# Expert slots: one PSUM bank after the other, and a new order of relu, split and load

## The chip, the cores and the metric

The program runs on one core of one Trainium2 chip, as one launch. A core has five engines with a queue each, worked through strictly in order: TensorE (PE; its weight loads are listed apart as PEld), VectorE (DVE), ScalarE (ACT), GpSimd (POOL) and SyncE (SP), which here issues most of the transfers. They wait for each other through semaphores. The metric is the device time of one execution in microseconds; lower is better.

## The reference, cut to what matters

Three layers follow each other: a chunked attention, a mixture of eight experts in which each token goes to one expert, and a dense layer with a rational activation. The change lies in the second:

```
logits = x @ w_gate + modality_bias[modality_id]      # 3072 tokens, 512 wide
e_idx = argmax(logits)
for e in range(8):                                    # only experts that have tokens
    mask = e_idx == e
    h = maximum(x[mask] @ w1[e], 0)                   # 512 -> 1024
    out[mask] = gate_w[mask, None] * (h @ w2[e])      # 1024 -> 512
...
h = x @ w_in; h2 = h * h; h3 = h2 * h                 # third layer, 512 -> 2048
P = a0 + a1 h + a2 h2 + a3 h3;  Q = 1 + |b0||h| + |b1| h2
return (P / (Q + 1e-6)) @ w_out                       # 2048 -> 512
```

## The kernel before, in words

**Slots.** The router sorts the tokens by expert and packs them into slots of 128; a slot belongs to one expert. Slots 0 and 1 are worked off in `second`, and the first product of slot 2 too; from then on the loop in `moe` runs passes i = 3 to 26. Pass i makes the first products of slot i (`mm1`), the hidden rows of slot i-1 (`prep_h`), and the second products and the output of slot i-1 (`mm2`, `out`). Slots 0 to 25 hold tokens.

**One pass on TensorE.** `mm1` multiplies 128 tokens (in two parts, `h` and `l`, high and low, so that the product keeps float32 precision) with `w1`, also in two parts, `w1h` and `w1l`: 24 matmuls of 128x512 into the two banks of the PSUM tile `pb`, both banks alternating. Between them stand the 8 transposes of `prep_h(i-1)`, which turn the relu'd rows `hs` for the second product. Then 4 transposes of `prep_x(i+1)`, the next slot's tokens, and 24 matmuls of `mm2(i-1)` into a bank of `pa`.

**The other engines in one pass.** ScalarE copies `prep_h`'s results to `hh`, makes the relu (`hs`, two halves, one a bank; every transpose of `prep_h` needs both), copies the next tokens (`xs`), and rounds new weights to their high part (`split_hi`, four pieces of 128x1024). VectorE makes the low parts (`hl`, `xs` low, `split_lo`). `out` scales the result on ScalarE.

**New weights.** When a slot's expert differs from that of the slot before it, `load_w` (SP, under an If on a flag) fetches four pieces of 512 KB into `w1r` or `w2r`, and `split_w` (ACT and DVE, under the same flag) makes the parts. `w1` of slot i+2 is asked for in pass i and split in pass i+1; `w2` of slot i is asked for in pass i and split in pass i+1. The next load into the same tile waits until the split has read it. In this data the expert changes at slots 12, 13 and 17; slot 12 is an expert with one slot.

**Filler.** The weights of the third layer are converted in 33 steps, hung into the passes: one step after `mm2` in each pass, a second one before `load_w(i, w2r)` while i < 12, the rest in pass 25. Step n splits piece n-1 (`pair`: a CAST on ACT to `wih` or `wo`, and a subtraction on DVE), asks on SP for piece n+1 into the half of `wr` that `pair` has just read, and works on piece n (`bits`: an ACTIVATE on ACT that waits for piece n to land, four instructions on DVE). The second kind of piece leaves through POOL to the tensor `wod`.

**The order** of every queue is that of the source (`manual_schedule`); the framework puts in the semaphores. In the last pass the first 512 result rows are prepared for the third layer (`Rows.prep`): two tiles of them through `pb`.

Of the kernel before, what the change touches and what calls it, by code (L numbers as in the profile page):

```python
# [12 lines left out]
F32 = mybir.dt.float32  # L13
# [33 lines left out]
def attention(nc, tc, ex, ident, q, k, v, wg_d, mod, mbias, pos_u, out_u, constants):  # L47
# [8 lines left out]
    with ExitStack() as ctx:  # L56
# [56 lines left out]

        def scores(t):
            qt, kt = qs[t % NB_IN], kz[t % NB_IN]
            sc = ex.pa[:, t % 2]
            for hp in range(HP):
                for c in range(TC):
                    x = c // 2 * KP + c % 2 * CH
                    nc.tensor.matmul(  # L120
                        sc[CH * c:CH * c + CH, hp * P:hp * P + P], lhsT=qt[:, hp, CH * c:CH * c + CH], rhs=kt[:, :, hp, x:x + 64],
                        start=True, stop=True,
                    )
            sc_t[t] = sc.rearrange("p (h k) -> p h k", k=64)
# [36 lines left out]
        def pv(t):  # L161
            s = pT_t.pop(t)
            w = vz[t % NB_IN]
            ps = ex.pb
            n = 2 * (D + 1)
            for hp in range(HP):
                for c in range(TC):
                    nc.tensor.matmul(
                        ps[CH * c:CH * c + CH, hp // 2, hp % 2 * n:hp % 2 * n + n], lhsT=s[:, hp, CH * c:CH * c + CH], rhs=w[:, :, hp, c, :],
                        start=True, stop=True,  # L170
                    )
            o = ps[:, :, 0:2 * n].rearrange("p g (h d) -> p g h d", d=D + 1)
            rs = wk.tile([P, 2, HP], F32, tag="rs", name="rs")
            V.tensor_scalar_add(rs, o[:, :, :, D], 1e-9)
            chore()
            V.reciprocal(rs, rs)
            chore()
            x = xp.tile([P, H, D], F32, tag="x", name="x")
            V.tensor_tensor(
                out=x.rearrange("p (g h) d -> p g h d", g=2), in0=o[:, :, :, 0:D],  # L180
                in1=rs[:, :, :, None].to_broadcast([P, 2, HP, D]), op=ALU.mult,
            )
            (nc.gpsimd if t < NT - 3 else nc.sync).dma_start(out=xd[row(t):row(t) + P, :], in_=x.rearrange("p h d -> p (h d)"))
            chore()
            x_t[t] = x
# [106 lines left out]
class Router:  # L292
# [226 lines left out]
    def second(self):  # L519
# [7 lines left out]
        ex.mm1_0(0, 3)  # L527
        ps = self.rank(n, NT)
        ex.prep_x0(1)
        ex.relu(0)  # L530
        ex.mm1_0(1, 0, 1, 2, 3)
        rest = self.first_rest()
        for f in rest[:2]:
# [47 lines left out]
        some = self.wk.tile([P, 32], F16, tag="rs", name="some")  # L581
        V.tensor_scalar(out=some, in0=tb, scalar1=0.0, scalar2=None, op0=ALU.not_equal)
        V.tensor_scalar(out=f[:, 1], in0=tb, scalar1=0.0, scalar2=-1.0, op0=ALU.is_gt, op1=ALU.mult)
        ex.relu(1)
        cnt = self.tp.tile([P, 32], F32, tag="t", name="cnt")
        ex.mm2_0(0, 0)
        nc.tensor.matmul(cnt, lhsT=self.ones, rhs=some, start=True, stop=True)
# [6 lines left out]
        ex.load_w(EARLY, ex.w1r, ex.w1v)  # L594
        ex.split_w(EARLY, ex.w1r, ex.w1h, ex.w1l)
        ex.load_w(EARLY + 1, ex.w1r, ex.w1v)
        for part in range(3):
            ex.mm1(EARLY, part)
            if part < 2:
                ex.prep_h0(1, part)  # L600
        for step in (*rest[2:], *self.terms(n, NT), *self.gates(n, NT), *self.gate_parts()):
            step()
        bg = self.wk.tile([P, NT, 3, 32], F16, name="bg", bufs=1)
# [1 line left out]
        V.tensor_tensor(  # L605
            out=bg, in0=be.rearrange("p s t -> p t s")[:, :, None, :].to_broadcast(SG), in1=self.g16[:, :, :, None].to_broadcast(SG), op=ALU.mult,
        )
        ex.relu(EARLY)
        low = ex.prep_x(EARLY + 1)
        ex.mm2_0(1, 0)  # L610
        low()
# [44 lines left out]
class Experts:  # L656


    def __init__(self, nc, tc, ident, xd, yd, w1, w2, src_u, pos_u, out_u, gate_s, flags):
        self.nc, self.tc, self.ident = nc, tc, ident  # L660
        self.xd, self.yd, self.src_u, self.pos_u, self.out_u, self.gate_s, self.flags = xd, yd, src_u, pos_u, out_u, gate_s, flags
        self.w1v = w1.rearrange("e (p k) f -> (e p) (k f)", k=4)
        self.w2v = w2.rearrange("e (p j) d -> (e p) (j d)", j=8)
        self.hps, self.yps, self.hT = {}, {}, {}
        self.ctx = ExitStack()
        self.sp = self.ctx.enter_context(tc.tile_pool(name="shared", side="right", bufs=1))
        self.ps = self.ctx.enter_context(tc.tile_pool(name="shared_ps", side="right", bufs=4, space=PSUM))
        self.pa = self.ps.tile([P, 2, 512], F32, name="pa", bufs=1)
        self.pb = self.ps.tile([P, 2, 512], F32, name="pb", bufs=1)
        self.hs = self.sp.tile([P, 8, P], F32, name="hs")  # L670
        self.xs = [self.sp.tile([P, 2, 4, P], F32R, name=f"xs{i}") for i in range(2)]
        self.xg = [self.sp.tile([P, D_M], F32, name=f"xg{i}") for i in range(3)]
        self.ys = self.sp.tile([P, D_M + 1], F32, name="ys")
        self.e0 = self.sp.tile([1, 1], I32, name="e0")
        self.w1r = self.sp.tile([P, 4, 1024], F32, name="w1r")
        self.w1h = self.sp.tile([P, 4, 1024], F32R, name="w1h")
        self.w1l = self.sp.tile([P, 4, 1024], F32R, name="w1l")
        self.w2r = self.sp.tile([P, 4, 1024], F32, name="w2r")
        self.xT = {}

    def open_w2(self, ctx):

        p = self.ctx.enter_context(self.tc.tile_pool(name="shared_w2", reuse_waits="tile", side="right", bufs=1))
        self.w2h = p.tile([P, 4, 1024], F32R, name="w2h")
        self.w2l = p.tile([P, 4, 1024], F32R, name="w2l")
# [53 lines left out]
        nc.vector.tensor_tensor(out=l, in0=ps, in1=h.bitcast(F32), op=ALU.subtract)  # L739

    def mm2(self, s, g):
        ps = self.pa[:, s % 2]
        for i, w in ((0, self.w2h), (1, self.w2h), (0, self.w2l)):
            for j in range(4):
                n = 4 * g + j
# [5 lines left out]
    def out(self, s, y=None):  # L751
        nc, y = self.nc, self.ys if y is None else y
        nc.gpsimd.tensor_copy(y[:, D_M:].bitcast(U32), self.out_u[:, s:s + 1])
        nc.scalar.activation(y[:, 0:D_M], self.pa[:, s % 2], func=AF.Copy, scale=self.gate_s[:, s:s + 1])
        nc.gpsimd.indirect_dma_start(
            out=self.yd, out_offset=bass.IndirectOffsetOnAxis(ap=self.pos_u[:, s:s + 1], axis=0), in_=y, in_offset=None,
            bounds_check=NT * P - 1, oob_is_err=False,
        )
# [8 lines left out]

    def mm1_0(self, s, *kks):
        if 0 in kks:
            self.hps[s] = [(self.pa if s == 0 else self.pb)[:, i] for i in range(2)]  # L770
        for kk in kks:
            for i in range(2):
                self.nc.tensor.matmul(
# [10 lines left out]
    def mm2_0(self, s, g):  # L784
        for n in range(4 * g, 4 * g + 4):
            self.nc.tensor.matmul(
                self.pa[:, s % 2], lhsT=self.h0[g][:, n % 4], rhs=self.w2r[:, n // 2, (n % 2) * 512:(n % 2) * 512 + 512],
                start=(n == 0), stop=(n == 7),
            )

    def relu(self, s):
        ps = self.hps.pop(s)
        for i in range(2):
            self.nc.scalar.activation(
                self.hs[:, :, i * 64:(i + 1) * 64].rearrange("p j q -> p q j"), ps[i].rearrange("p (q j) -> p q j", j=8), func=AF.Relu,
            )

    def prep_x(self, s):

# [6 lines left out]
        self.xT[s] = (h, l)  # L806
        return lambda: nc.vector.tensor_tensor(out=l, in0=ps, in1=h.bitcast(F32), op=ALU.subtract)

    def mm1(self, s, part):
        h, l = self.xT[s]  # L810
        w1h, w1l = self.w1h, self.w1l
        if part == 0:
            self.hps[s] = [(self.pa if s == 0 else self.pb)[:, i] for i in range(2)]
        ps = self.hps[s]
        products = [(x, w1h, kk) for kk in (2 * part, 2 * part + 1) for x in (h, l)] if part < 2 else [(h, w1l, kk) for kk in range(4)]
        for x, w, kk in products:
            for i in range(2):
                self.nc.tensor.matmul(  # L818
                    ps[i], lhsT=x[:, kk, :], rhs=w[:, kk, i * 512:(i + 1) * 512],
                    start=(x is h and w is w1h and kk == 0), stop=(w is w1l and kk == 3),  # L820
                )


NM = NT + 2
# [2 lines left out]
def moe(nc, tc, ex, filler, rows):  # L827
# [4 lines left out]
    gather, load_w, split_w, mm1, relu, prep_h, mm2, out = ex.gather, ex.load_w, ex.split_w, ex.mm1, ex.relu, ex.prep_h, ex.mm2, ex.out  # L832
    for i in range(EARLY + 1, NM + 1):

        if i < NM:
            if i + 2 < NM:
                gather(i + 2)
            for part in range(3):
                mm1(i, part)
                if part < 2:  # L840
                    prep_h(i - 1, part)
            split_w(i - 1, w2r, w2h, w2l)
            relu(i)
            if i + 1 < NM:
                ex.prep_x(i + 1)()
        else:
            for g in range(2):
                prep_h(i - 1, g)
            split_w(i - 1, w2r, w2h, w2l)
        if i < 12:  # L850
            filler()
        if i < NM:
            load_w(i, w2r, w2v)
        if i == NM - 1:
            while filler():
                pass
# [3 lines left out]
                rows.load(t, w1r[:, t, 0:D_M + 1])  # L860
        if i == NM:
            for t in range(4):
                ps = ex.ps.tile([P, 4, P], F32, tag="t", name="yps") if t < 2 else ex.pb[:, t - 2].rearrange("p (k n) -> p k n", k=4)
                rows.prep(t, w1r[:, t, 0:D_M + 1], ps, rows.h, rows.l)

        if i + 1 < NM:
            split_w(i + 1, w1r, w1h, w1l)
        if i + 2 < NM:
            load_w(i + 2, w1r, w1v)
        for part in range(2):  # L870
            mm2(i - 1, part)
        filler()
# [3 lines left out]
    with tc.If(more == 1):  # L876
        for i in range(NM, NS):
# [5 lines left out]
            with tc.If(used == 1):  # L883
                gather(i)
                ex.prep_x(i)()
                for part in range(3):
                    mm1(i, part)
                relu(i)
                prep_h(i, 0)
                prep_h(i, 1)  # L890
                for part in range(2):
# [343 lines left out]
```

## Time and profile before

| what | us |
|---|---|
| median of three runs | 1014.68 (1013.2 to 1015.07) |
| the profiled execution | 1013.12 |
| its span | 1011.3 |
| TensorE busy in the span | 973.5 (96%) |
| VectorE, ScalarE busy | 750.5 (74%), 592.2 (59%) |

The page's table in 40 slices of 25.3 us shows TensorE busy at 9 tenths or more in 35 of them; the others are the first (5), the last (6) and those that begin at 76, 126 and 430 us (8). The passes of the expert loop begin at 155.61 us (pass 3) and end at 461.71 us, where the third layer begins. "idle before <-releaser" in the rows below is the time for which an engine had nothing to run, and the instruction that ended it; "SPq" is a transfer's issue on SP, not its end.

### The profile page before, as it was taken

What the parts mean: (1) busy time and instruction counts of PE and PEld (TensorE: products, weight loads), DVE (VectorE), ACT (ScalarE), POOL (GpSimd) and SP (SyncE); (2) the same over time, 40 slices, a digit from 0 to 9 for tenths busy, and PEclk for the clock granted to TensorE, in tenths of its full rate; (3) what the DMA queues carried; (4) which work ended last, traced back from release to release, by engine and by line L of the source; (5) the groups of instructions that cost most, each with busy time, mean ns of one, the idle gap of its engine ahead of it and who ended that gap; (6) DMA issues with size and microseconds to landing.
All of it is one profiled execution on the core that took longest, in us unless ns stands there. A gap on an engine that the chain in (4) does not pass through costs nothing.

```text
span 1011.3 us, 16205 instructions
## 1 busy us (share of the span) xinstructions
PE 973.5 (96%) x5809; PEld 780.0 (77%) x5809; DVE 750.5 (74%) x1217; ACT 592.2 (59%) x947; POOL 147.3 (15%) x205
## 2 busy tenths in 40 slices
PE   5998989999999999989999999999999999999996
PEld 4776557888778888867888888888888888888885
DVE  5767455666685553345998889988888888889885
ACT  2443435555575554445776666766676666667663
POOL 5112013111143333220000100100020001001001
PEclk9999999999999999999999999999999999999999
DMA  8999322443686643346130101000010001001001
GB/s 262 364 382 388 135 74 73 127 125 107 214 306 219 236 151 126 115 147 234 53 111 11 42 11 32 32 10 21 22 43 11 22 11 42 21 1 42 1 1 42
DMA packets 37993, 110.43 MB, mean 109 GB/s; under 512 B 6950, under 2 KB 6978, under 8 KB 37892
## 3 DMA queue, kind: packets, MB, share of 16 engines
q1 hardware_dynamic: 27540, 76.43, 22.1%
q0 software_dynamic: 10352, 32.79, 9.1%
q8 instruction: 47, 0.77, 0.3%
q14 instruction: 54, 0.44, 0.1%
HBM read 82.44 MB, written 27.80 MB: 109 GB/s over the span
## 4 chain that ended last, share of the span: by engine, by line
PE 54%; POOL 0%; POOLq 0%; DVE 0%; issue 0%
PE a L1108 9%; PE a L1106 9%; PE a L1107 9%; PE h L1054 9%; PE h L1053 9%; PE h L1052 9%; PE yps L936 1%; POOL out L1118 0%; POOLq L1231 0%; DVE o L1116 0%; POOLq L1118 0%
## 5 line engine op out<-in xcount | busy, mean ns | idle before, releaser
L1052 PE MATMUL h<-yh,wih 128*128 128x512 f32 x384 | 151.7, 395 | 0.4 <-PEq L876 0.4
L1108 PE MATMUL a<-wo,gl 128*128 128x512 f32 x384 | 151.9, 396 | 0.0
L1106 PE MATMUL a<-wo,gh 128*128 128x512 f32 x384 | 151.9, 396 | 0.0
L1107 PE MATMUL a<-wo,gh 128*128 128x512 f32 x384 | 151.9, 395 | 0.0
L1054 PE MATMUL h<-yh,wil 128*128 128x512 f32 x384 | 150.6, 392 | 0.0
L1053 PE MATMUL h<-yl,wih 128*128 128x512 f32 x384 | 150.3, 391 | 0.0
L1064 ACT ACTIVATE s<-h 128x512 f32<-128x512 f32 x96 | 57.5, 599 | 140.4 <-PE h L1054 140.3
L1071 DVE SCALAR_TENSOR_TENSOR q<-s,absb,q 128x512 f32<-128x512 f32 x96 | 72.0, 750 | 44.6 <-ACT q L1065 44.6
L818 PE MATMUL pb<-w1h,xs 128*128 128x512 f32 x384 | 101.7, 407 | 2.4 <-ACT w1h L719 2.4
L1108 PEld LDWEIGHTS a<-wo,gl 128*128 128x128 f32 x384 | 72.2, 188 | 17.6 <-DVE gl L1094 0.3
L818 PEld LDWEIGHTS pb<-w1h,xs 128*128 128x128 f32 x384 | 71.2, 191 | 18.8 <-ACT w1h L719 2.8
L1107 PEld LDWEIGHTS a<-wo,gh 128*128 128x128 f32 x384 | 72.2, 188 | 16.9
L1052 PEld LDWEIGHTS h<-yh,wih 128*128 128x128 f32 x384 | 72.2, 188 | 16.6 <-issue 0.8
L1106 PEld LDWEIGHTS a<-wo,gh 128*128 128x128 f32 x384 | 72.2, 188 | 16.5
L1053 PEld LDWEIGHTS h<-yl,wih 128*128 128x128 f32 x384 | 72.2, 188 | 15.7
L1054 PEld LDWEIGHTS h<-yh,wil 128*128 128x128 f32 x384 | 72.1, 188 | 15.7
L1066 ACT ACTIVATE u<-h,ab 128x512 f32<-128x512 f32 x96 | 75.1, 782 | 0.0
L1084 DVE SCALAR_TENSOR_TENSOR u<-u,ab,q 128x512 f32<-128x512 f32 x96 | 72.2, 752 | 3.4
L1073 DVE SCALAR_TENSOR_TENSOR u<-u,ab,h 128x512 f32<-128x512 f32 x96 | 71.8, 748 | 3.4
L1082 DVE SCALAR_TENSOR_TENSOR q<-q,cb,s 128x512 f32<-128x512 f32 x96 | 71.6, 746 | 0.1
L1077 ACT ACTIVATE s<-q,cb 128x512 f32<-128x512 f32 x96 | 70.6, 735 | 0.7 <-DVE q L1071 0.2
L1083 DVE SCALAR_TENSOR_TENSOR q<-q,s 128x512 f32<-128x512 f32 x96 | 66.4, 692 | 3.3
(227 smaller groups left out, 1720.4 us busy)
## 6 DMA issues: line engine op xcount, KB each, us to landing
v<-in_v SPq DMA_DIRECT2D x48, 260.0 KB
w1r<-in_moe_w SPq DMA_DIRECT2D x16, 512.0 KB
w2r<-in_moe_w SPq DMA_DIRECT2D x16, 512.0 KB
wr<-in_moe_w_in SPq DMA_DIRECT2D x16, 512.0 KB
wr<-in_moe_w_out SPq DMA_DIRECT2D x16, 512.0 KB
wod<-wo POOLq DMA_DIRECT2D x32, 256.0 KB
wo<-wod SPq DMA_DIRECT2D x16, 512.0 KB
k<-in_k SPq DMA_DIRECT2D x48, 168.0 KB
```

The source lines that it names most:

```text
L818: self.nc.tensor.matmul(ps[i], lhsT=x[:, kk, :], rhs=w[:, kk, i * 512:(i + 1) * 512], start=(x is h and w is w1h and kk == 0), stop=(w is ...
L1052: nc.tensor.matmul(ps, lhsT=wih[k][:, sl], rhs=h[:, k], start=(k == 0), stop=False)
L1053: nc.tensor.matmul(ps, lhsT=wih[k][:, sl], rhs=l[:, k], start=False, stop=False)
L1054: nc.tensor.matmul(ps, lhsT=wil[k][:, sl], rhs=h[:, k], start=False, stop=(k == NK - 1))
L1066: A.activation(u, ps, func=AF.Identity, scale=a3, bias=a2)
L1071: V.scalar_tensor_tensor(out=q, in0=s, scalar=absb1, in1=q, op0=ALU.mult, op1=ALU.add)
L1073: V.scalar_tensor_tensor(out=u, in0=u, scalar=a1, in1=ps, op0=ALU.add, op1=ALU.mult)
L1082: V.scalar_tensor_tensor(out=q, in0=q, scalar=cb, in1=s, op0=ALU.add, op1=ALU.mult)
L1084: V.scalar_tensor_tensor(out=u, in0=u, scalar=a0, in1=q, op0=ALU.add, op1=ALU.mult)
L1106: nc.tensor.matmul(ps, lhsT=gh[:, sl], rhs=wo[f][:, 0].bitcast(F32R), start=(f == 0), stop=False)
L1107: nc.tensor.matmul(ps, lhsT=gh[:, sl], rhs=wo[f][:, 1].bitcast(F32R), start=False, stop=False)
L1108: nc.tensor.matmul(ps, lhsT=gl[:, sl], rhs=wo[f][:, 0].bitcast(F32R), start=False, stop=(f == NF - 1))
```

## The change

The two PSUM tiles of two banks become tiles of one bank (`pa[0]`, `pa[1]`, `pb[0]`, `pb[1]`); the attention's use of `pb` gets a tile of its own, `pv`, closed before `pb` is opened. `mm1` takes a bank and a half of its twelve products; `relu` takes a bank. The pass is written in a new order, and the filler's second step stands in passes up to 13.

```diff
     def mm1(self, s, i, part):
         h, l = self.xT[s]
-        products = [(x, w1h, kk) for kk in (2 * part, 2 * part + 1) for x in (h, l)] if part < 2 else [(h, w1l, kk) for kk in range(4)]
-        for x, w, kk in products:
-            for i in range(2):
-                self.nc.tensor.matmul(
-                    ps[i], lhsT=x[:, kk, :], rhs=w[:, kk, i * 512:(i + 1) * 512],
+        products = [(x, self.w1h, kk) for kk in range(4) for x in (h, l)] + [(h, self.w1l, kk) for kk in range(4)]
+        for n in range(6 * part, 6 * part + 6):
+            x, w, kk = products[n]
+            self.nc.tensor.matmul(
+                self.hps[s][i], lhsT=x[:, kk, :], rhs=w[:, kk, i * 512:(i + 1) * 512], start=(n == 0), stop=(n == 11),
...
     for i in range(EARLY + 1, NM + 1):
+        split_w(i - 1, w2r, w2h, w2l)
+        for g in range(2):
+            if i < NM:
+                mm1(i, 0, g)
+            prep_h(i - 1, g)
         if i < NM:
             if i + 2 < NM:
                 gather(i + 2)
-            for part in range(3):
-                mm1(i, part)
-                if part < 2:
-                    prep_h(i - 1, part)
-            split_w(i - 1, w2r, w2h, w2l)
-            relu(i)
+            relu(i, 0)
+            for part in range(2):
+                mm1(i, 1, part)
             if i + 1 < NM:
                 ex.prep_x(i + 1)()
-        else:
-            for g in range(2):
-                prep_h(i - 1, g)
-            split_w(i - 1, w2r, w2h, w2l)
-        if i < 12:
-            filler()
-        if i < NM:
+                split_w(i + 1, w1r, w1h, w1l)
+            relu(i, 1)
+            if i < 14:
+                filler()
             load_w(i, w2r, w2v)
+            if i + 2 < NM:
+                load_w(i + 2, w1r, w1v)
...
-        if i + 1 < NM:
-            split_w(i + 1, w1r, w1h, w1l)
-        if i + 2 < NM:
-            load_w(i + 2, w1r, w1v)
         for part in range(2):
             mm2(i - 1, part)
         filler()
         out(i - 1)
```

SP's queue, from the end of pass 11 into pass 12, before: `wr` is a filler's piece (asked for after `mm2` of pass 11), `w2r` the new second weights of slot 12.

```order
L955 DMA wr<-in_moe_w_out 128x1024
L713 TENSOR_LOAD flags
L713 ISA x2
L714 TENSOR_LOAD flags
L714 ISA x2
L727 UNCONDITIONAL_BRANCH
L715 COMPARE_AND_BRANCH
L704 ISA
L704 DMA w2r<-in_moe_w 128x1024
```

The same place after the change:

```order
L957 DMA wr<-in_moe_w_out 128x1024
L735 UNCONDITIONAL_BRANCH x2
L957 DMA wr<-in_moe_w_out 128x1024
L721 TENSOR_LOAD flags
L721 ISA x2
L722 TENSOR_LOAD flags
L722 ISA x2
L723 COMPARE_AND_BRANCH
L712 ISA
L712 DMA w2r<-in_moe_w 128x1024
```

In passes 12 and 13 a filler's piece has moved in ahead of the load of `w2r`; it is the piece that waits for that step's `pair`.

ScalarE's queue in pass 12, before: `hh` is `prep_h(11)`, `hs` the two halves of relu 12, `xs` the tokens of slot 13, `wo` the filler's `pair`.

```order
L738 CAST hh_1831<-hTp 128x512
L738 CAST hh_1833<-hTp 128x512
...
L719 CAST w2h<-w2r 128x1024 x4
...
L794 ACTIVATE hs<-pb 128x64x8 x2
L805 CAST xs_85<-xps 128x512
...
L719 CAST w1h<-w1r 128x1024 x4
...
L968 CAST wo<-wr 128x512
```

The same place after:

```order
L727 CAST w2h<-w2r 128x1024 x4
...
L746 CAST hh_1841<-hTp 128x512
L746 CAST hh_1843<-hTp 128x512
L800 ACTIVATE hs<-pb_1834 128x64x8
L811 CAST xs_89<-xps 128x512
...
L727 CAST w1h<-w1r 128x1024 x4
...
L800 ACTIVATE hs<-pb_1835 128x64x8
L970 CAST wo<-wr 128x512
```

The split of `w2` has moved ahead of both copies of `prep_h`, and the split of the next `w1` ahead of the second half of the relu.

## Rows read from the trace of the kernel before

**Rows 1.** Waits of PE in the expert passes: us in total, times, longest.
```profile
PE pb L936 <- DVE yl L939: 4.2, 1, 4.2
PE pb L818 <- ACT w1h L719: 2.4, 1, 2.4
```
**Rows 2.** Timeline of PE: start, us, line, tiles, count, idle before.
```profile
242.91 2.02 PE L818 MATMUL pb<-w1h,xs 128*128 128x512 f32 x8
...
255.32 2.02 PE L818 MATMUL pb<-w1h,xs 128*128 128x512 f32 x8
...
262.17 1.17 PE L746 MATMUL pa<-w2h,hh 128*128 128x512 f32 x4
...
270.28 3.54 PE L818 MATMUL pb<-w1h,xs 128*128 128x512 f32 x8 [2.38 <-ACT w1h L719]
...
284.26 2.02 PE L818 MATMUL pb<-w1h,xs 128*128 128x512 f32 x8
...
310.71 2.02 PE L818 MATMUL pb<-w1h,xs 128*128 128x512 f32 x8
```
**Rows 3.** Timeline of ACT in passes 11 to 14.
```profile
262.04 2.01 ACT L794 ACTIVATE hs<-pb 128x512 f32<-128x512 f32 x2 [1.28 <-issue]
...
268.52 0.66 ACT L910 ACTIVATE wf<-wr 128x512 f32<-128x512 f32 x1 [3.50 <-DMA wr<-in_moe_w_out]
269.18 3.89 ACT L719 CAST w1h<-w1r 128x1024 fp32r<-128x1024 f32 x4
...
294.15 1.05 ACT L719 CAST w2h<-w2r 128x1024 fp32r<-128x1024 f32 x1 [0.82 <-SPq L715]
...
303.53 4.06 ACT L719 CAST w2h<-w2r 128x1024 fp32r<-128x1024 f32 x4 [0.18 <-ACT hh L738]
```
**Rows 4.** Timeline of DVE in pass 12.
```profile
271.48 4.62 DVE L722 TENSOR_TENSOR w1l<-w1r,w1h 128x1024 fp32r<-128x1024 f32 x4
276.02 0.68 DVE L969 TENSOR_TENSOR wo<-wr,wo 128x512 fp32r<-128x512 f32 x1
...
278.87 1.28 DVE L739 TENSOR_TENSOR hl<-hTp,hh 128x512 fp32r<-128x512 f32 x2
```
**Rows 5.** Timeline of SP's transfers in passes 10 to 13: start and length of the issue.
```profile
253.40 0.33 SPq L955 DMA_DIRECT2D wr<-in_moe_w_in  x1
256.98 2.36 SPq L704 DMA_DIRECT2D w1r<-in_moe_w  x4
261.00 5.16 SPq L955 DMA_DIRECT2D wr<-in_moe_w_out  x2
...
280.41 4.87 SPq L704 DMA_DIRECT2D w2r<-in_moe_w  x4
...
296.51 3.30 SPq L704 DMA_DIRECT2D w2r<-in_moe_w  x4
```
**Rows 6.** Stretches: window, length, busy PE, PEld, DVE, ACT, POOL, PEclk, DMA share, GB/s.
```profile
257.00:267.00 10.00, 10.00 (x51) 8.34 (x50) 4.77 (x9) 5.29 (x8) 2.24 (x2) 1.00 0.86 297
...
270.00:272.00 2.00, 1.72 (x4) 1.43 (x5) 1.93 (x4) 2.00 (x3) 0.00 (x0) 0.50 0.00 0
455.00:457.00 2.00, 2.00 (x6) 1.56 (x5) 0.54 (x1) 0.00 (x0) 0.00 (x0) 0.50 0.01 4
```
**Rows 7.** Timelines of PE and DVE at the end of the passes.
```profile
447.03 1.03 PE L736 MATMUL hTp<-ident,hs 128*128 128x128 f32 x8
447.90 1.04 PE L936 MATMUL yps<-ident,w1r 128*128 128x128 f32 x8
...
453.54 0.66 PE L936 MATMUL pb<-ident,w1r 128*128 128x128 f32 x4 [4.16 <-DVE yl L939]
...
461.71 0.47 PE L1052 MATMUL h<-yh,wih 128*128 128x512 f32 x1 [0.45 <-PEq L876]
...
451.60 1.29 DVE L939 TENSOR_TENSOR yl<-yps,yh 128x512 fp32r<-128x512 f32 x2 [1.16 <-DMA wod<-wo]
```
**Rows 8.** Waits of PE in the attention, the one of the score products for DVE.
```profile
PE pa L120 <- DVE rs L174: 0.3, 1, 0.3
```

More of the change, by code (lines that the diff above doesn't have):

```diff
@@ L115, in scores @@
             qt, kt = qs[t % NB_IN], kz[t % NB_IN]
-            sc = ex.pa[:, t % 2]
+            sc = ex.pa[t % 2]
             for hp in range(HP):
@@ L163, in pv @@
             w = vz[t % NB_IN]
-            ps = ex.pb
+            ps = ex.pv
             n = 2 * (D + 1)
@@ L529, in second @@
         ex.prep_x0(1)
-        ex.relu(0)
+        for i in range(2):
+            ex.relu(0, i)
         ex.mm1_0(1, 0, 1, 2, 3)
@@ L583, in second @@
         V.tensor_scalar(out=f[:, 1], in0=tb, scalar1=0.0, scalar2=-1.0, op0=ALU.is_gt, op1=ALU.mult)
-        ex.relu(1)
+        for i in range(2):
+            ex.relu(1, i)
         cnt = self.tp.tile([P, 32], F32, tag="t", name="cnt")
@@ L596, in second @@
         ex.load_w(EARLY + 1, ex.w1r, ex.w1v)
-        for part in range(3):
-            ex.mm1(EARLY, part)
-            if part < 2:
-                ex.prep_h0(1, part)
+        for part in range(2):
+            ex.mm1(EARLY, 0, part)
+            ex.prep_h0(1, part)
+        ex.relu(EARLY, 0)
+        for part in range(2):
+            ex.mm1(EARLY, 1, part)
         for step in (*rest[2:], *self.terms(n, NT), *self.gates(n, NT), *self.gate_parts()):
@@ L607, in second @@
         )
-        ex.relu(EARLY)
+        ex.relu(EARLY, 1)
         low = ex.prep_x(EARLY + 1)
@@ L667, in __init__ @@
         self.ps = self.ctx.enter_context(tc.tile_pool(name="shared_ps", side="right", bufs=4, space=PSUM))
-        self.pa = self.ps.tile([P, 2, 512], F32, name="pa", bufs=1)
-        self.pb = self.ps.tile([P, 2, 512], F32, name="pb", bufs=1)
+        self.pa = [self.ps.tile([P, 512], F32, name=f"pa{i}", bufs=1) for i in range(2)]
+        self.pvx = ExitStack()
+        self.pv = self.pvx.enter_context(tc.tile_pool(name="a_pv", side="right", bufs=1, space=PSUM)).tile([P, 2, 512], F32, name="pv")
         self.hs = self.sp.tile([P, 8, P], F32, name="hs")
@@ L681, in open_w2 @@
     def open_w2(self, ctx):
+        self.pvx.close()
+        p = self.ctx.enter_context(self.tc.tile_pool(name="shared_h", reuse_waits="tile", side="right", bufs=1, space=PSUM))
+        self.pb = [p.tile([P, 512], F32, name=f"pb{i}") for i in range(2)]
         p = self.ctx.enter_context(self.tc.tile_pool(name="shared_w2", reuse_waits="tile", side="right", bufs=1))
@@ L741, in mm2 @@
     def mm2(self, s, g):
-        ps = self.pa[:, s % 2]
+        ps = self.pa[s % 2]
         for i, w in ((0, self.w2h), (1, self.w2h), (0, self.w2l)):
@@ L753, in out @@
         nc.gpsimd.tensor_copy(y[:, D_M:].bitcast(U32), self.out_u[:, s:s + 1])
-        nc.scalar.activation(y[:, 0:D_M], self.pa[:, s % 2], func=AF.Copy, scale=self.gate_s[:, s:s + 1])
+        nc.scalar.activation(y[:, 0:D_M], self.pa[s % 2], func=AF.Copy, scale=self.gate_s[:, s:s + 1])
         nc.gpsimd.indirect_dma_start(
@@ L769, in mm1_0 @@
         if 0 in kks:
-            self.hps[s] = [(self.pa if s == 0 else self.pb)[:, i] for i in range(2)]
+            self.hps[s] = self.pa if s == 0 else self.pb
         for kk in kks:
@@ L786, in mm2_0, with relu @@
             self.nc.tensor.matmul(
-                self.pa[:, s % 2], lhsT=self.h0[g][:, n % 4], rhs=self.w2r[:, n // 2, (n % 2) * 512:(n % 2) * 512 + 512],
+                self.pa[s % 2], lhsT=self.h0[g][:, n % 4], rhs=self.w2r[:, n // 2, (n % 2) * 512:(n % 2) * 512 + 512],
                 start=(n == 0), stop=(n == 7),
             )
-    def relu(self, s):
-        ps = self.hps.pop(s)
-        for i in range(2):
-            self.nc.scalar.activation(
-                self.hs[:, :, i * 64:(i + 1) * 64].rearrange("p j q -> p q j"), ps[i].rearrange("p (q j) -> p q j", j=8), func=AF.Relu,
-            )
+    def relu(self, s, i):
+        self.nc.scalar.activation(
+            self.hs[:, :, i * 64:(i + 1) * 64].rearrange("p j q -> p q j"), self.hps[s][i].rearrange("p (q j) -> p q j", j=8), func=AF.Relu,
+        )
     def prep_x(self, s):
@@ L807, in prep_x, with mm1 @@
         return lambda: nc.vector.tensor_tensor(out=l, in0=ps, in1=h.bitcast(F32), op=ALU.subtract)
-    def mm1(self, s, part):
+    def mm1(self, s, i, part):
         h, l = self.xT[s]
[L811 to L814, printed above, removed]
-        products = [(x, w1h, kk) for kk in (2 * part, 2 * part + 1) for x in (h, l)] if part < 2 else [(h, w1l, kk) for kk in range(4)]
-        for x, w, kk in products:
-            for i in range(2):
-                self.nc.tensor.matmul(
-                    ps[i], lhsT=x[:, kk, :], rhs=w[:, kk, i * 512:(i + 1) * 512],
-                    start=(x is h and w is w1h and kk == 0), stop=(w is w1l and kk == 3),
-                )
+        if i == part == 0:
+            self.hps[s] = self.pa if s == 0 else self.pb
+        products = [(x, self.w1h, kk) for kk in range(4) for x in (h, l)] + [(h, self.w1l, kk) for kk in range(4)]
[3 more added lines that the diff above has]
+                self.hps[s][i], lhsT=x[:, kk, :], rhs=w[:, kk, i * 512:(i + 1) * 512], start=(n == 0), stop=(n == 11),
+            )
 NM = NT + 2
@@ L837, in moe @@
                 gather(i + 2)
-            for part in range(3):
-                mm1(i, part)
-                if part < 2:
-                    prep_h(i - 1, part)
-            split_w(i - 1, w2r, w2h, w2l)
-            relu(i)
+            relu(i, 0)
+            for part in range(2):
+                mm1(i, 1, part)
             if i + 1 < NM:
                 ex.prep_x(i + 1)()
-        else:
-            for g in range(2):
-                prep_h(i - 1, g)
-            split_w(i - 1, w2r, w2h, w2l)
-        if i < 12:
-            filler()
-        if i < NM:
+                split_w(i + 1, w1r, w1h, w1l)
+            relu(i, 1)
+            if i < 14:
+                filler()
             load_w(i, w2r, w2v)
+            if i + 2 < NM:
+                load_w(i + 2, w1r, w1v)
         if i == NM - 1:
@@ L862, in moe @@
             for t in range(4):
-                ps = ex.ps.tile([P, 4, P], F32, tag="t", name="yps") if t < 2 else ex.pb[:, t - 2].rearrange("p (k n) -> p k n", k=4)
+                ps = ex.ps.tile([P, 4, P], F32, tag="t", name="yps") if t < 2 else ex.pb[t - 2].rearrange("p (k n) -> p k n", k=4)
                 rows.prep(t, w1r[:, t, 0:D_M + 1], ps, rows.h, rows.l)
-        if i + 1 < NM:
-            split_w(i + 1, w1r, w1h, w1l)
-        if i + 2 < NM:
-            load_w(i + 2, w1r, w1v)
         for part in range(2):
@@ L885, in moe @@
                 ex.prep_x(i)()
-                for part in range(3):
-                    mm1(i, part)
-                relu(i)
+                for g in range(2):
+                    for part in range(2):
+                        mm1(i, g, part)
+                    relu(i, g)
                 prep_h(i, 0)
```

## The prediction

> **What bounds the kernel now.** I read the page's busy times first: TensorE works in 96% of the span, so an edit gains only where PE stands, and loses wherever it makes PE stand. The chain of waits agrees: it runs through PE. Then PE's waits in the expert passes [rows 1]: beyond a few tenths there are two, 2.4 us for the split of new first weights and 4.2 us at the end for `yl`. PE's timeline shows the rest. A pass without new weights takes 255.32 - 242.91 = 12.41 us [rows 2], with `mm2` 6.85 us into it (262.17) and 5.56 us long, 0.232 a product. PE waits for no relu and no copy in such a pass: ScalarE waits for it (1.28 before `hs` [rows 3]). So making the relu start a bank earlier gains nothing there. From pass 11 to the start of pass 15 (255.32 to 310.71) PE needs 55.39 us instead of 4 x 12.41 = 49.64: new weights cost 5.75, of it the wait of 2.38 ahead of pass 12. Pass 12 then takes 284.26 - 270.28 = 13.98, 1.57 too long, because after the wait the granted clock is 0.50 (1.2 GHz) [rows 6]. From 447.03 the last pass takes 14.68 us to the third layer [rows 7], with the wait for `yl` and once more a clock of 0.50 behind it [rows 6].
>
> **Durations that I use.** ScalarE or VectorE on 128x512: 0.65 (0.66, 0.68, 1.28 for two); relu of a bank 1.0 (2.01 for both); split of a piece 1.0 on ScalarE (3.89 for four); the filler's four instructions on VectorE 2.2 (from the end of the 276.02 row to 278.87) [rows 3, 4]. A lone 512 KB piece: SP's next transfer follows 4.0 us after the load's first issue (256.98 to 261.00), which I read as the first piece's landing [rows 5]. A load of four: in pass 11 five pieces had landed 11.54 us after 256.98 (ScalarE goes on at 268.52 with the fifth, issued behind them); with the first at 4.0 that is 1.9 apiece, the fourth at 9.7. The one of 296.51 had landed by the fourth CAST, 303.53 + 3 x 1.0 = 306.5, so in 10.0 at most; the one of 280.41, which overlaps another load, took 13.7 (294.15) [rows 3, 5]. I take 10.0, and 13.7 as the upper end; a lower end follows with the rivals. A check of a load's flag on SP takes (256.98 - 253.73)/2 = 1.6 [rows 5].
>
> **The change, part by part.** *A. Ahead of pass 12: -2.4.* The filler's ACTIVATE that held up ScalarE's split for 3.50 us [rows 3] now stands behind the split. The last piece of `w1` (slot 12) lands at 256.98 + 10.0 = 267.0, its high part is ready at 268.0, and the relu's second bank, now behind it, at 269.0. Pass 12 starts on time at 255.32 + 12.41 = 267.7, and its first transposes, six products later (1.4), need that relu at 269.1. Nothing is lost.
>
> *B. Behind it: +2.25.* In pass 11 the filler's pair follows that relu: CAST to 269.65, subtraction to 270.3, and only then SP asks for the next piece, which lands at 274.3. The filler behind `mm2` waits for it on ScalarE, and behind that ACTIVATE (274.95) stand the output copy (275.6) and the first `hh` of slot 11 (276.25). `mm2` is due at 267.7 + 6.85 = 274.6: 1.65 late. VectorE's filler ends at 277.15 and `hl` at 277.8, 0.6 after the four products that can go before it. Pass 13 starts at 282.4.
>
> *C. The next `w1`: +1.75.* On SP the load for slot 13 comes after that same piece and two checks: 270.3 + 3.25 = 273.55. It lands at 283.55, is split by 284.55, and the relu of slot 12's second bank, which has no need of it but stands behind it in ScalarE's queue, ends at 285.55. The transposes are due at 282.4 + 1.4 = 283.8.
>
> *D. The `w2` of slot 12: +9.1.* This load used to go out at 280.41 [rows 5]. Now a filler's piece stands ahead of it on SP, which waits for the pair, which waits for that relu: 286.2, 286.85, check 288.45, landed 298.45, split 299.45. The split also stands ahead of both copies to `hh` now, so the first `hh` comes at 300.1 instead of beside the load; `mm2` is due 5.45 after the transposes, at 291.0. PE stands 9.1 us, and about 0.35 more for `hl`. Pass 14 starts at 306.0.
>
> *E. The `w2` of slot 13: +5.1.* The same round again: second `hh` 300.75, relu 301.75, `xs` 302.4, relu 303.4, pair 304.7, check 306.3, landed 316.3, split 317.3, `hh` 317.95, against 306.0 + 6.85 = 312.85. With 0.35 for `hl` and 1.57 of slow clock (as after the wait of 2.38; behind B to D the next transfer's wait swallows it) pass 15 starts at 306.0 + 12.41 + 5.1 + 0.35 + 1.57 = 325.4, where it was 310.71: **+14.7**.
>
> *F. Slot 17: 0.* Its pass has no filler ahead of the load any more in either kernel (both limits lie below 17), so the load goes out as early as before.
>
> *G. The end: -6.1.* `pb` is now two tiles, so the last four transposes need not wait until `yl` has read the other bank. `yl` itself waited 1.16 for a filler's transfer [rows 7]; with two steps in passes 3 to 13 the 33 steps end in pass 24 (11 x 2 + 11), before it. What remains: 24 transposes at 0.87 for eight (447.03 to 447.90), 5.56 of `mm2` and 0.45 of branch, 8.6 instead of 14.68. Late next is `yl`, four subtractions behind `hl`, some 453.0 on the old scale, needed at 455.6. If another wait takes the place of the one for `yl`, the gain is down to 0; I take it whole, because I find no other instruction that PE would wait for there.
>
> *Without a price.* The order bank by bank: `mm2` sends 24 products into one bank at the same 0.232 as `mm1` into two. Conversely nothing is won by it. The attention's own tile `pv` could save the 0.3 of [rows 8] at most, or cost as much; 0. Two more early filler pieces and two fewer late ones: behind PE in passes without new weights.
>
> The sum: 14.7 - 6.1 = +8.6 on the profiled execution's 1013.12, 1021.7. The median of the runs is 1.56 above that execution, so I forecast 1023.3.
>
> **Rivals.** The sum hangs on three loads in a row (C, D, E), each of which now waits for the one before it through relu, pair and SP; one us less of each moves the end by 3 us, and the sum is 0 at a load of 10.0 - 8.6/3 = 7.1 us.
> (1) *Short loads.* What was measured at 10.0 shared the DMA engines with the filler's pieces and the token transfers: 297 GB/s and a share of 0.86 [rows 6]. If a load that is alone ends 4.0 after its last issue (256.98 + 2.0 + 4.0), it takes 6.0: 8.6 - 12 = -3.4, 1011.3, faster. Against it: fillers' pieces and tokens stand beside it now too.
> (2) *Middling loads.* At 8 us the sum is 8.6 - 6 = +2.6, 1017.3. For it: between the 6.0 and the 10.0. The Trainium skill, DMA: Bandwidth & Descriptors, Specifications, gives about 358 GB/s as the limit of a core's HBM traffic, and its section Anatomy of one DMA a fixed cost of about 2.0 us; for 2.1 MB that makes 5.9 + 2.0 = 7.9 us, an estimate from that page, by which the sum would be +2.3; the rows above stand at 9.7 to 10.0 with other traffic beside them.
> (3) *Long loads.* At 13.7 the sum is 8.6 + 11.1 = +19.7, 1034.4. Against it: that load overlapped another, and C to E follow each other.
> (4) *The change does only what it says*, with no new wait: -5.75 - 6.1, 1002.8. It needs `w2` of slot 12 to go out near 281 still, which the order on SP excludes unless the fillers run far ahead of where I put them.
>
> **How the numbers follow.** Forecast 0.65, with its own range 1019 to 1029.4 (loads of 9 to 10, and the end without its gain); (2) 0.16; (3) 0.07; (1) 0.06; a load near 7.1, no change, 0.04; (4) 0.02. Within 0.2% is about what a measurement of this kernel can tell from no change. So faster is 0.08, the same 0.04, slower 0.65 + 0.16 + 0.07 = 0.88. A range of 1015.5 to 1030 holds the forecast and (2) and leaves out 0.19.
>
> **What would show it.** Right: passes 3 to 10 still 12.41; no wait for `w1h` ahead of pass 12; SP's load of `w2` for slot 12 near 288 instead of 280; PE idle some 9 us before `mm2` of slot 12, released by the copy to `hh` behind the split, then some 5 us before that of slot 13; from the last eight `hTp` transposes to the third layer 8.6 us. Wrong: no idle time of PE over 3 us in passes 13 to 15, or a new wait in passes without new weights, or a wait for `yl` that is still there.

## The result, and the profile after

| | before | after |
|---|---|---|
| median, us | 1013.94 | 1026.11 (1022.8 to 1029.08) |
| the profiled execution, its span | 1013.12, 1011.3 | 1025.48, 1023.7 |
| pass 11 to the start of pass 15 | 55.39 | 75.63 |
| last `hTp` transposes to the third layer | 14.68 | 8.76 |

The changed kernel is slower by a ratio of 1.0118 (95% interval 1.0099 to 1.0138), 12.2 us; the forecast was 1023.3 with a range of 1015.5 to 1030. Waits of PE in the passes after, in all, times, longest:

```profile
PE pa L754 <- ACT hh L746: 14.4, 3, 8.8
...
PE pb L823 <- ACT w1h L727: 1.7, 1, 1.7
PE hTp L744 <- ACT hs L800: 1.6, 1, 1.6
PE pa L754 <- DVE hl L747: 0.9, 1, 0.9
```

Against [rows 1] the wait for `yl` is gone, and the copies to `hh` have taken the first place, in three waits. Where they stand, in PE's timeline (start, us, line, tiles, count, idle before); pass 11 begins at 253.92, pass 14 at 309.46, pass 15 at 329.55:

```profile
253.92 1.56 PE L823 MATMUL pb<-w1h,xs 128*128 128x512 f32 x6
...
266.31 1.56 PE L823 MATMUL pb<-w1h,xs 128*128 128x512 f32 x6
...
273.83 1.19 PE L754 MATMUL pa<-w2h,hh 128*128 128x512 f32 x4 [0.47 <-ACT hh L746]
275.93 1.19 PE L754 MATMUL pa<-w2h,hl 128*128 128x512 f32 x4 [0.91 <-DVE hl L747]
...
283.39 0.74 PE L823 MATMUL pb<-w1h,xs 128*128 128x512 f32 x2 [1.69 <-ACT w1h L727]
285.75 1.12 PE L744 MATMUL hTp<-ident,hs 128*128 128x128 f32 x4 [1.62 <-ACT hs L800]
...
301.86 2.08 PE L754 MATMUL pa<-w2h,hh 128*128 128x512 f32 x4 [8.85 <-ACT hh L746]
...
309.46 1.56 PE L823 MATMUL pb<-w1h,xs 128*128 128x512 f32 x6
...
321.61 2.07 PE L754 MATMUL pa<-w2h,hh 128*128 128x512 f32 x4 [5.10 <-ACT hh L746]
...
329.55 1.56 PE L823 MATMUL pb<-w1h,xs 128*128 128x512 f32 x6
...
465.36 1.03 PE L744 MATMUL hTp<-ident,hs 128*128 128x128 f32 x8
...
474.12 0.47 PE L1054 MATMUL h<-yh,wih 128*128 128x512 f32 x1 [0.51 <-PEq L877]
```

Pass 12 starts 12.39 after pass 11, without the wait of 2.38 in [rows 2]. Then come the steps B, C, D and E of the prediction in their order. The loads behind them, in SP's timeline after, answering to [rows 5]:

```profile
271.93 2.69 SPq L712 DMA_DIRECT2D w1r<-in_moe_w  x4
277.22 10.01 SPq L957 DMA_DIRECT2D wr<-in_moe_w_out  x2
289.22 2.06 SPq L712 DMA_DIRECT2D w2r<-in_moe_w  x4
...
308.46 2.05 SPq L712 DMA_DIRECT2D w2r<-in_moe_w  x4
```

what SP waited for between 250 and 332 us (its pieces of the filler for the subtraction of a `pair`, in three waits):

```profile
SPq L957 <- DVE wo L971: 15.0, 3, 7.8
```

and the split of each load's last piece with what follows, in ScalarE's timeline:

```profile
283.68 1.05 ACT L727 CAST w1h<-w1r 128x1024 fp32r<-128x1024 f32 x1 [0.35 <-DMA w1r<-in_moe_w]
284.64 1.06 ACT L800 ACTIVATE hs<-pb 128x512 f32<-128x512 f32 x1
285.49 0.65 ACT L970 CAST wo<-wr 128x512 fp32r<-128x512 f32 x1
...
300.28 1.04 ACT L727 CAST w2h<-w2r 128x1024 fp32r<-128x1024 f32 x1 [1.04 <-SPq L723]
301.23 1.06 ACT L746 CAST hh<-hTp 128x512 fp32r<-128x512 f32 x2
...
320.03 1.04 ACT L727 CAST w2h<-w2r 128x1024 fp32r<-128x1024 f32 x1 [0.84 <-SPq L723]
```

From the first issue to the start of the last piece's split, which I take for its landing (before the two of `w2` the view names SP's branch, `SPq L723`, as what came last), the loads took 283.68 - 271.93 = 11.75, 300.28 - 289.22 = 11.06 and 320.03 - 308.46 = 11.57 us. What the DMA engines moved meanwhile (window, length, busy PE, PEld, DVE, ACT, POOL, PEclk, DMA share, GB/s), answering to [rows 6]:

```profile
271.90:283.70 11.80, 8.74 (x38) 6.51 (x37) 6.91 (x10) 6.79 (x10) 3.22 (x4) 1.00 0.93 311
289.20:300.30 11.10, 3.81 (x21) 3.12 (x19) 6.42 (x8) 5.07 (x7) 3.56 (x5) 0.80 0.86 317
308.50:320.00 11.50, 8.01 (x41) 6.50 (x40) 6.17 (x8) 5.00 (x6) 3.55 (x5) 0.99 0.83 303
302.00:304.00 2.00, 2.00 (x5) 1.61 (x6) 2.00 (x4) 1.88 (x4) 0.00 (x0) 0.50 0.47 182
```

The rate is close to that of [rows 6] (297), but 3.5 to 3.7 MB went by (311 x 11.8), of which the load is 2.1; in [rows 6] it was 3.0. The last row is the clock of 0.50 behind the wait of 8.85.

### The profile page after: what moved, and what is told of

Its sections match the earlier page's. It is cut to its first block, busy times and chain, and to the rows that moved or that the text cites. A ratio compares the mean times of both kernels' runs of the same rounds, so it can differ in the third digit from the quotient of the medians.

```text
span 1023.7 us, 16164 instructions
## 1 busy us (share of the span) xinstructions
PE 975.9 (95%) x5809; PEld 782.7 (76%) x5809; DVE 753.1 (74%) x1217; ACT 595.4 (58%) x947; POOL 145.7 (14%) x205
## 4 chain that ended last, share of the span: by engine, by line
PE 53%; POOL 0%; POOLq 0%; DVE 0%; issue 0%
PE a L1110 9%; PE a L1108 9%; PE a L1109 9%; PE h L1056 9%; PE h L1055 9%; PE h L1054 9%; PE yps L938 1%; POOL out L1120 0%; POOLq L1233 0%; DVE o L1118 0%; POOLq L1120 0%
## 5 line engine op out<-in xcount | busy, mean ns | idle before, releaser
L823 PE MATMUL pb<-w1h,xs 128*128 128x512 f32 x384 | 106.0, 408 | 1.7 <-ACT w1h L727 1.7
L823 PEld LDWEIGHTS pb<-w1h,xs 128*128 128x128 f32 x384 | 68.7, 189 | 15.2 <-ACT w1h L727 2.1
L754 PE MATMUL pa<-w2h,hh 128*128 128x512 f32 x192 | 55.8, 413 | 14.4 <-ACT hh L746 14.4
```

The source lines that it names most:

```text
L823: self.nc.tensor.matmul(self.hps[s][i], lhsT=x[:, kk, :], rhs=w[:, kk, i * 512:(i + 1) * 512], start=(n == 0), stop=(n == 11),)
```

## The experiments

Theory: three loads in a row, each held up by relu, filler's pair and SP's queue, cost the time, and the end of the passes gives some back through the tiles. Rivals: the order of split and copies alone; the order bank by bank; an end that gains by the fillers.

**The filler's limit undone.**

```diff
-            if i < 14:
+            if i < 12:
                 filler()
```

> The changed kernel with the filler's second step again only in passes up to 11 (i < 12 instead of i < 14), all else as changed. Theory (three loads in a row, each held up by relu, pair and SP): in passes 12 and 13 no piece stands ahead of the load of w2 on SP any more, so w2 of slot 12 goes out at about 281 to 283 us instead of 289.22 and PE's wait before mm2 of slot 12 falls from 8.85 to about 4 us, that of slot 13 from 5.10 to about 2 or less; about 10 us below the changed kernel, 1016 (1012 to 1019). Rival (the order of split and copies alone is the loss, the load's time does not matter): the two waits stay within 2 us of what they were, 1022 or more. Both: the end of the passes keeps its 8.7 us, unless the filler's last step, now in pass 25, brings back a wait for yl.

Measured: 1010.18, ratio to before 0.9966 (0.9953 to 0.9979): 16 us below the changed kernel, more than expected, and faster than before. SP and PE, the loads of `w2` and what is left of PE's waits:

```profile
279.83 6.06 SPq L712 DMA_DIRECT2D w2r<-in_moe_w  x4
294.50 2.28 SPq L712 DMA_DIRECT2D w2r<-in_moe_w  x4
```

```profile
284.44 0.74 PE L823 MATMUL pb<-w1h,xs 128*128 128x512 f32 x2 [1.86 <-ACT w1h L727]
286.96 1.11 PE L744 MATMUL hTp<-ident,hs 128*128 128x128 f32 x4 [1.78 <-ACT hs L800]
```

With `w2` asked for at 279.83 instead of 289.22 both waits for `hh` in D and E are gone, with the split still ahead of the copies; C is left (pass 13 takes 19.35 instead of 28.86, pass 14 12.38 instead of 20.09). The edit also takes the step's own work off ScalarE and VectorE in these two passes; this run doesn't separate that from the place on SP, and the chain from relu over `pair` to the load is read from the changed kernel's rows above. The end keeps its gain with the filler's last step in pass 25 (20.8 from pass 25 to the third layer, 20.6 in the changed kernel).

**The split of `w2` back behind the copies.**

```diff
-        split_w(i - 1, w2r, w2h, w2l)
         for g in range(2):
...
             prep_h(i - 1, g)
+        split_w(i - 1, w2r, w2h, w2l)
```

> The changed kernel with the split of w2 moved back behind the copies of prep_h (split_w(i - 1) after both prep_h), all else as changed, the load still behind the filler's piece. Theory: the load goes out at 289 as before, so most of the loss stays; but hh is ready early and mm2 of slot 12 can start once two pieces are split, some 4 us before 301.86, and then waits for the later pieces; 4 to 7 us below the changed kernel in all, 1019 to 1022. Rival (the order of split and copies alone is the loss): both waits are gone, 1008 or less.

Measured: 1019.24 (1.0051, 1.0035 to 1.0068), 6.9 below the changed kernel. PE no longer waits for the whole split and then the copies, but for one piece after the other:

```profile
299.16 0.73 PE L754 MATMUL pa<-w2h,hh 128*128 128x512 f32 x2 [1.94 <-ACT w2h L727]
301.04 1.22 PE L754 MATMUL pa<-w2h,hh 128*128 128x512 f32 x2 [1.14 <-ACT w2h L727]
...
317.11 0.72 PE L754 MATMUL pa<-w2h,hh 128*128 128x512 f32 x2 [2.32 <-ACT w2h L727]
318.95 1.22 PE L754 MATMUL pa<-w2h,hh 128*128 128x512 f32 x2 [1.12 <-ACT w2h L727]
```

So the place of the split decides how much of a late load PE feels, and the late load itself is the larger part: this edit leaves 5 us of loss, the one before none.

**Loads of two pieces.** The kernel leaves out half of the weights in every load from slot 12 on.

```diff
-            self.load(e, raw, view)
+            for i in range(2 if s > 11 else 4):
+                nc.sync.dma_start(out=raw[:, i], in_=view[bass.ds(e * P, P), i * 1024:(i + 1) * 1024])
```

> The changed kernel with only the first two of four pieces fetched in the loads of slots from 12 on (the products of these slots use old weights in the other two pieces). Theory: each load in the chain (w1 of slot 13, w2 of 12, w2 of 13) is shorter by two pieces at 2 us, 4 us, and the end moves by the sum of the three, 8 to 12 us below the changed kernel, 1014 to 1018. Rival (the chain is held by relu, pair and SP, and the load's length is hidden): less than 3 us below, 1023 or more.

Measured: 1017.01 (1.0032, 1.0015 to 1.0048), 9.1 below the changed kernel. Shorter loads alone, with order and fillers as changed, take 9.1 of the 12.2 us back; the last piece fetched lands after 7.6, 6.7 and 6.8 us, 13.3 less in three, and two more CASTs, 1.9 us, still follow each.

**The tiles alone**, on the kernel before; e6 is a second execution of the program of e4:

> The kernel before with only the PSUM tiles changed: pa and pb as tiles of one bank, the attention's pv of its own; order, relu and fillers as before. Theory: the wait of 4.16 us for yl at the end of the passes, and the slow clock behind it (about 1.9), come from pb being one tile, so both go: 4 to 6 us below before, 1008 to 1010, and the passes 11 to 14 as before. Rival (the end gains because the filler's steps end in pass 24 instead of 25): no gain, 1013 to 1015, and PE still waits about 4 us there, for yl or for the transfer of a filler.

> The kernel before with only the tiles of one bank, a second profile: whether the 2.78 us for which PE stood behind the first product of the third layer, waiting for nothing that the profile shows, come again. Theory (a chance of that execution, as they aren't there in the changed kernel): under 1 us. Rival (it belongs to this program): 2 us or more again.

Measured: 1012.63, ratio 0.999 (0.9973 to 1.0006), no difference that these runs can tell and less than the 1008 to 1010 expected; the second execution 1013.86. The wait for `yl` is gone in both (from pass 25 to the third layer 20.96 and 20.83 instead of 26.59, a gain of 5.6 to 5.8), so that it came from the tiles of two banks is shown. But in the two profiles most is lost again behind the first product of the third layer, in the first execution and in the second:

```profile
454.30 0.47 PE L1056 MATMUL h<-yh,wih 128*128 128x512 f32 x1 [0.82 <-ACT ys L758]
457.56 0.40 PE L1057 MATMUL h<-yl,wih 128*128 128x512 f32 x1 [2.78 <-issue]
```

```profile
458.20 0.47 PE L1056 MATMUL h<-yh,wih 128*128 128x512 f32 x1 [0.68 <-PEq L880]
461.38 0.58 PE L1057 MATMUL h<-yl,wih 128*128 128x512 f32 x1 [2.71 <-issue]
```

"issue" is time in which PE waited for nothing that the profile shows. It came again, so a chance of one execution is unlikely: it seems to belong to this program. With a clock of 0.50 behind it the third layer takes 554 us instead of 549.6.

**The gain of step A alone**, on the kernel before:

```diff
+        if i + 1 < NM:
+            split_w(i + 1, w1r, w1h, w1l)
         if i < 12:
             filler()
```

> The kernel before with one edit: the split of the next w1 stands ahead of the filler's second step instead of behind it; order, relu, tiles and fillers else as before. Theory (a gain at pass 12 is given back by the next loads): PE's wait ahead of pass 12 (2.4 us and its slow clock) is gone, but the filler's pair and with it SP's next piece and the loads behind it come later, so passes 12 to 14 grow by as much; 1013 to 1016, no gain. Rival (the wait that is removed is time saved): 1010 or less, with passes 12 to 14 at about 12.4 to 13.4 us.

Measured: 1013.84, ratio 0.9993 (0.9978 to 1.0008), no gain. Pass 11 takes 12.41 instead of 14.96, but passes 12 to 14 take 16.08, 14.33 and 12.70 instead of 13.98, 13.41 and 13.04: from pass 11 to pass 15 55.5 against 55.4. In ScalarE's queue the price is seen, and in PE's the wait that it makes:

```profile
274.28 0.65 ACT L968 CAST wo<-wr 128x512 fp32r<-128x512 f32 x1 [3.58 <-DVE wr L914]
275.65 0.67 ACT L910 ACTIVATE wf<-wr 128x512 f32<-128x512 f32 x1 [0.72 <-DMA wr<-in_moe_w_out]
276.23 0.67 ACT L754 ACTIVATE ys<-pa,gate_s 128x512 f32<-128x512 f32 x1
276.80 1.06 ACT L738 CAST hh<-hTp 128x512 fp32r<-128x512 f32 x2
...
277.96 1.96 PE L746 MATMUL pa<-w2h,hh 128*128 128x512 f32 x4 [1.82 <-ACTq L727]
```

The filler now stands with its waits between the split and `hh`, which is late for `mm2` (1.8 us of PE): step B, and time saved ahead of pass 12 is given back behind it.

**No filler in passes 11 to 13**, in the old order with the new tiles, and in the new order with the split of `w2` behind the copies (the lines are those of the new order; the old one had `i < 12`):

```diff
-            if i < 14:
+            if i < 11 or 17 < i < 23:
                 filler()
...
-        filler()
+        if not 10 < i < 14:
+            filler()
         out(i - 1)
```

> The old order of the pass, with the tiles of one bank, and no filler step at all in passes 11 to 13 (a second step in passes up to 10 and in passes 18 to 22 instead, so that all 33 are done). Theory (the fillers in the passes of the expert change hold up splits and loads, and the order bank by bank gives nothing): pass 12 starts on time and passes 11 to 14 take about 50 us together instead of 55.4; with the end 9 to 11 us below before, 1003 to 1006. Rival (the loads are too late for the old order anyway, it needs the new one): waits of 2 us and more for w1h or w2h stay, 1008 or more.

> The changed kernel with no filler step in passes 11 to 13 (a second step up to pass 10 and in passes 18 to 22 instead) and with the split of w2 behind the copies of prep_h. Theory: no load stands behind a filler's piece, no wait over 1 us in passes 11 to 15, end of 8.7 us kept; 1002 to 1004, within 2 us of the same fillers in the old order. Rival (bank by bank is worth something by itself): 3 us or more below the old order with the same fillers.

Measured: 1006.94 in the old order (0.991, 0.9882 to 0.9939), 1002.99 in the new (0.9881, 0.9854 to 0.9907). From pass 11 to pass 15 they take 50.3 and 49.6 us, so the loads are in time in either order once no filler holds them up. The median of the new order is 3.95 lower, against "within 2 us", but the two intervals overlap and little of it is seen in the passes: 0.8 in this stretch, 0.4 in passes 18 and 19, 0.02 in each steady pass (12.39 against 12.41). The old order shows the wait of "issue" again, in a profiled execution (1011.07) that is the slowest of its six:

```profile
PE h L1058 <- issue: 2.3, 1, 2.3
```

**That wait by itself**: the old order as above, with 16 transposes more on PE ahead of the third layer, whose result nothing reads.

> The old order with the tiles of one bank and no filler in passes 11 to 13, as run before, plus 16 more transposes on PE in the last pass whose result nothing reads, so that PE's program ahead of the third layer is 16 products longer (some 1.3 us of work). Theory (the 2.3 to 2.8 us behind the first product of the third layer, which three kernels with the old order and the new tiles showed, hang on where that product stands in PE's program): the wait goes, and the third layer takes 549.6 us again instead of 554 to 555; in all 2 to 4 us below the run without the 16. Rival (they hang on the old order or on the tiles): the wait stays, and the time is 1 us longer.

Measured: 1006.18 (0.9925, 0.9907 to 0.9943). In its profiled execution (1003.76) the wait is gone and the third layer takes 1002.0 - 452.37 = 549.6 us:

```profile
PE h L1060 <- PEq L884: 0.7, 1, 0.7
```

But the median is only 0.8 below that without the 16, not 2 to 4, and the intervals overlap. That the wait hangs on where the product stands in PE's program fits the profiles; its worth in the median isn't shown, and its cause is open.

**The second steps moved back**: `19 < i < 25` instead of `17 < i < 23`, in the new order.

> The changed order with no filler step in passes 11 to 13, the split of w2 behind the copies of prep_h, and the filler's five second steps in passes 20 to 24 instead of 18 to 22. Theory: pass 18, which took 13.61 us because a filler's piece behind the load of slot 17 came late, takes 12.4; 1.0 to 1.3 us below the same with the steps in 18 to 22, about 1002. Rival (the length of pass 18 comes from the load of w2 itself): no change.

Measured: 1002.14 (0.9881, 0.9864 to 0.9899). The long pass (it is pass 19, not 18 as the expectation counted) takes 12.39 instead of 13.62. But the end pays for it: from pass 25 to the third layer PE takes 22.5 instead of 20.8 us and waits for the rows that are loaded for the third layer:

```profile
PE pb L939 <- DMA w1r<-yd: 1.4, 2, 0.7
```

So no gain from the move is shown; the medians differ by 0.85, too little to tell from their spread. It has the lowest median: 12.3 below before, 24 below the changed kernel.

## Why the prediction was right

The steps on one scale, us after the start of pass 11 (253.92 after, 255.32 in the sum):

| step | predicted | measured |
|---|---|---|
| A: pass 12 starts | 12.4 | 12.39 |
| B: pass 13 starts | 27.1 | 26.68 |
| C: first transposes of pass 13 | 30.2 | 31.83 |
| D: load of `w2` (12) asked for | 33.1 | 35.30 |
| D: its `mm2` | 44.8 | 47.94 |
| pass 14 starts | 50.7 | 55.54 |
| E: load of `w2` (13) asked for | 51.0 | 54.54 |
| E: its `mm2` | 62.6 | 67.69 |
| pass 15 starts | 70.1 | 75.63 |
| G: what the end gives back | -6.1 | -5.9 |

**A** came as predicted, and e5 shows it is worth nothing alone. **B** came with 0.47 and 0.91 of wait; 1.9 us late against 2.25. **C** cost PE more than its 1.75: two waits of 1.69 and 1.62, and slow clock behind them. **C, D, E** are the chain that was forecast, with PE idle 8.85 (9.1) and 5.10 (5.1), released by `hh` behind the split. That these two agree so well is in part luck: the copies came 3.2 and 5.1 us later than forecast, but PE, held up in C and slow behind its waits, was ready for `mm2` 3.4 and 5.1 us later too. Undoing the fillers' part of it (e1) removes D and E, and shorter loads (e3) shrink the whole.

What was mis-sized is the load, "I take 10.0": 11.75, 11.06 and 11.57, 4.4 us more in three. That is most of the 5.5 by which pass 15 came later than forecast; the rest is some 0.8 on the way to the loads and 0.5 of slow clock behind the last wait. [Rows 5] gave 9.7 beside 0.9 MB of other traffic, and at most 10.0 beside 1.0; here 1.4 to 1.6 MB shared the engines. Whose they were, the transfers by queue tell (packets, MB, share of the engines' time), in the stretch of [rows 6] before and in that of the first load after:

```profile
q1 hardware_dynamic: 680, 2.52, 74.4%
q0 software_dynamic: 127, 0.45, 11.1%
```

```profile
q1 hardware_dynamic: 707, 2.58, 65.5%
q0 software_dynamic: 320, 1.05, 26.5%
```

The first queue is SP's, with the load and the filler's pieces, and moved as much as before. The 0.6 MB on top are in POOL's (1.09 and 1.02 beside the two other loads). That is the filler's second kind of piece on its way to `wod`, two transfers of 256 KB a step: POOL issued none of them in the stretch of [rows 6], and after the change a pair at the start of the first load and two pairs from 3 us ahead of each of the others on. The prediction counted pieces and tokens beside a load, not these, and read its 9.7 from the last load before they began. That they made the loads longer fits the bytes, but no run leaves them out.

The rivals with shorter loads therefore leaned the wrong way. The estimate of 7.9 us, worked out from the Trainium skill, DMA: Bandwidth & Descriptors (Specifications, and Anatomy of one DMA, which gives its fixed cost for a transfer that GpSimd issues, while these are SyncE's), was too short for want of bytes. With all that went by, 3.5 to 3.7 MB, the same estimate comes to 11.7 to 12.3 us, 0.2 to 0.8 above what each load took here.

The factor of 3 a microsecond was right in kind: in e3 the three loads, with the CASTs that still follow, end 13.3 - 3 x 1.9 = 7.6 us earlier, and pass 15 starts 66.2 instead of 75.6 after pass 11; of the remaining 1.9 the last `mm2` makes up 1.5: behind a wait of only 1.40 it takes 6.45 instead of 7.94 us.

**F** held (passes 17 to 19 take 12.4 us each). **G** held with its cause: the tiles remove the wait for `yl`; e1 keeps the gain with the filler's last step in pass 25, so the two earlier steps, the sum's other reason, weren't needed in the new order. What has no price in the sum, the order bank by bank, may be worth something: with no filler in its way the new order as a whole (e8 against e7) saves about 1.5 us in the passes. What the banks alone do in it isn't separated.

Not in the sum: pass 11 started 1.40 earlier than before. Both executions wait 2.4 us for `bg` shortly before pass 3; in the one before the clock fell behind it, in the one after it didn't (the windows below, of before and of after; from the products behind that wait to pass 3 6.18 and 4.64 us). This is a difference of executions, not of the change: e4 and e6, one program, take 4.64 and 6.33 us there.

```profile
150.50:153.50 3.00, 3.00 (x14) 1.74 (x13) 0.38 (x2) 0.24 (x1) 0.00 (x0) 0.50 0.00 0
```

```profile
150.50:153.50 3.00, 3.00 (x22) 1.80 (x21) 0.39 (x2) 0.93 (x2) 0.00 (x0) 1.00 0.00 0
```

So it is partly luck that the median came only 2.8 us above the forecast, with pass 15 5.5 later than forecast. These 1.4, passes 15 to 25 with 0.5 less, and a median 0.63 above the profiled execution, where the sum had taken 1.56, made up for about half. A small slip in the working: loads of 9 us give 1020.3, not the 1019 that the forecast's own range begins with; no conclusion hangs on it.

## What to carry to other kernels

When work is moved ahead of a load in the queue that issues it, follow what that work itself waits for: here a filler's piece tied SP to a relu, and each load to the one before, so that a microsecond more of load counted once for each of the three. A wait removed ahead of one pass is a gain only if the work that caused it isn't put in front of the next one. Time a load with all the bytes that share the DMA engines while it is under way, not with its own.

## What the runs showed that was not expected

Three executions of two programs stood 2.3 to 2.8 us behind the first product of the third layer for nothing that the profile shows; with 16 products more ahead of it, in one profiled execution, it was gone. That PE waited there for its own instructions is an untested rival: the queues that the profile calls "instruction" moved three packets in the 3.1 us behind that product with the wait (e6) and without it (e9) alike, so the profile doesn't settle it. The same wait of 2.4 us can leave the clock at 1.00 or bring it to 0.50 in two executions, worth 1.5 us.
